# Two linear-attention branches with a gate: the first loads put in one queue, and two input tiles turned before the first product

## The chip, the cores and the metric

The kernel runs on one core of one Trainium2 chip. A core has five engines with a program of their own each: PE (TensorE, matmuls and transposes), DVE (VectorE), ACT (ScalarE), POOL (GpSimd) and SP (SyncE, which here does nothing but issue transfers). Loads and stores are issued from an engine's instruction stream into that engine's own queue; SP's queue is q1 in the profile and ACT's is q10. The packets of both are moved by the same 16 DMA engines. The metric is the device time of one execution in microseconds, as the median of several runs.

## The reference

Two branches A and B have weights of their own and share the input x (2048 rows of 640). Each is a linear attention with 32 heads of 20 columns; a gate mixes the two results.

```
qkv = x @ wqkv                       # 640 -> 3*640, for each branch
pq, pk = phi(q), phi(k)              # phi(t) = (t + 1 if t > 0 else exp(t)) + 1e-6
kv  = sum over s of pk[s] x v[s]     # per head, 20 x 20
z   = sum over s of pk[s]
o   = (pq . kv) / (pq . z + 1e-6)
branch = o @ wo
out = sigmoid((x * gate_w).sum(-1)) * A + (1 - sigmoid(...)) * B
```

## The kernel before

The 2048 rows of x are 16 row tiles of 128, and the 640 columns are 5 column blocks of 128. `XN` holds x as it lies in memory, `XT` holds it transposed (columns on the partitions), and `WK` holds the K part of `wqkv`. K of a row tile is the sum over the five column blocks c of `XT[c, tile]` times `WK[c]`: ten matmuls, a wide one of 512 columns and a narrow one of 128 for each block.

Every piece of work is entered once into a list by helper functions (`dma`, `mms`, `act`, `dve`, `pool`), and each engine then runs its own entries in the order of the list. What an entry reads and writes is declared, and the waits between engines are worked out from that. So the order in the source is the order of every engine and of every DMA queue, and an instruction that waits holds back all that stands behind it on its engine.

The part that the change touches is the start.

- **The loads, L380 to L408.** For the row tiles t = 0 to 3, `load_xn` puts 128 rows of x (160 KB) into SP's queue and `load_wk` puts block t of A's K weights (160 KB) into ACT's queue. Behind them SP's queue gets block 4 of A's K weights, all of B's K weights (800 KB), one column of gate weights, and then fifteen transposing transfers: five column blocks for each of the row groups 4 to 7, 8 to 11 and 12 to 15, which write `XT` directly. The weights of Q and V and the rest of `XN` follow. All transfers are issued at L293.
- **The transposes of the first four tiles.** They are not made by a transfer but on PE: `turn(t, b0)` (L426) waits for `XN` of tile t, makes five PE transposes (L436) into the PSUM banks b0 and b0 + 1, and lets DVE copy column blocks 0 to 2 (L450) and ACT blocks 3 and 4 (L448) into `XT`.
- **The first products.** `ks((t, c), ...)` (L840) adds column block c to K of row tile t through `k_part`: two matmuls a unit, at L304 like all products. Tile t collects in the PSUM pair t, that is in banks 2t and 2t + 1. `fill(bk, n, w)` (L418) makes n matmuls of w columns on constants, whose results nobody reads.
- **The order at the start, L844 to L863.** Twelve fill matmuls, `turn(0)`, one more fill, then products and turns of the tiles 1 to 3 in turn, the remaining products tile by tile, and then `k_tile` for each of the four tiles, which evicts K: ACT takes the exponential (L489) and DVE finishes phi (L500, L505). After that come B's K for the tiles 0 to 3, A's for 4 to 7, B's for 4 to 7 and so on, the Q products, the sums over rows, and the output products with the stores.

The first of A's products for tile 4 needs all five transposing transfers of the row group 4 to 7.

Of the kernel before, what the change touches and what calls it, by code (L numbers as in the profile page):

```python
# [8 lines left out]
ACT = mybir.ActivationFunctionType  # L9
# [197 lines left out]
def bass_gated_mix__linear_attn_block__linear_attn_block__prompt_kernel(  # L207
# [18 lines left out]
    with ExitStack() as es:  # L226
# [45 lines left out]
        def bank(i, lo, hi, p0=0, p1=128):  # L272
            o = 512 * (i % 2)
            return PP[i // 2][p0:p1, o + lo : o + hi]
# [10 lines left out]
        def dma(eng, name, o_ap, i_ap, reads=(), writes=(), transpose=False, noncontig=None):  # L285
            sem = new_sem(name)

            def fn(engobj):
                if noncontig is not None:
                    with nc.allow_non_contiguous_dma(reason=noncontig):  # L290
                        ins = engobj.dma_start(o_ap, i_ap, transpose=transpose)
                else:
                    ins = engobj.dma_start(o_ap, i_ap, transpose=transpose)  # L293
                return ins.then_inc(sem, 16)

            return sch.op(eng, fn, reads=reads, writes=writes, name=name, sem=sem, total=16)

        def mms(steps, reads=(), writes=(), name=""):


            def fn(pe):
                ins = None
                for o, l, r, st, sp, tp in steps:
                    ins = pe.matmul(o, l, r, start=st, stop=sp, tile_position=tp)  # L304
                return ins

            return sch.op("PE", fn, reads=reads, writes=writes, name=name)
# [5 lines left out]
        def act(fn, reads=(), writes=(), name=""):  # L313
            return sch.op("ACT", fn, reads=reads, writes=writes, name=name)

        def dve(fn, reads=(), writes=(), name=""):
            return sch.op("DVE", fn, reads=reads, writes=writes, name=name)
# [7 lines left out]
        def load_xn(eng, t0, t1):  # L325
            dma(
                eng,
                "xn%d" % t0,
                XN[:, t0:t1, :],
                xin[128 * t0 : 128 * t1, :].rearrange("(t p) f -> p t f", p=128),  # L330
                writes=[("XN", t) for t in range(t0, t1)],
            )
# [18 lines left out]
        def load_wk(eng, X, c0, c1):  # L351
            dma(
                eng,
                "wk%s%d" % (X, c0),
                WK[X][:, c0:c1, 0:D],
                wqkv[X][128 * c0 : 128 * c1, D : 2 * D].rearrange("(c p) f -> p c f", p=128),
                writes=[("WK", X, c) for c in range(c0, c1)],
            )
# [10 lines left out]
                fill=0.0,  # L369
# [7 lines left out]
            lambda e: e.activation(SG[:, 2, 0:1], nc.const_aps.tensor(1.0, (128, 1), dt.float32), ACT.Exp),  # L377
            writes=[("SGE", 0)],
        )
        for t in range(4):  # L380
            load_xn("SP", t, t + 1)
            load_wk("ACT", "A", t, t + 1)
        load_wk("SP", "A", 4, NC)
        load_wk("SP", "B", 0, NC)
        dma(
# [35 lines left out]
        def fill(bk, n, w=512):  # L421
            mms(
                [(bank(bk, 0, w), C1[:, 0:128], C1[:, 0:w], True, True, None)] * n,
                writes=[("PS", bk)],
                name="fill",
            )  # L426

        def turn(t, b0):
            for cs, bk in (((0, 1, 2), b0), ((3, 4), b0 + 1)):
                n = len(cs)  # L430
                dst = bank(bk, 0, 64 * n).bitcast(dt.bfloat16)

                def tr(pe, dst=dst, cs=cs):
                    ins = None
                    for i, c in enumerate(cs):
                        ins = pe.transpose(  # L436
                            dst[:, 128 * i : 128 * i + 128],
                            XN[:, t, 128 * c : 128 * c + 128],
                            IDN[:, :],
                        )  # L440
                    return ins

                sch.op("PE", tr, reads=[("XN", t), ("IDN",)], writes=[("PS", bk)], name="tr%d" % t)
                o = XT[:, cs[0] : cs[0] + n, 128 * t : 128 * t + 128]
                i = dst.rearrange("p (c s) -> p c s", c=n)
                ks = [("XT", t, c) for c in cs]
                if n == 2:
                    act(lambda e, o=o, i=i: e.activation(o, i, ACT.Copy), reads=[("PS", bk)], writes=ks)  # L448
                else:
                    dve(lambda e, o=o, i=i: e.tensor_copy(o, i), reads=[("PS", bk)], writes=ks)  # L450
# [4 lines left out]
        def k_part(X, t, pp, cs, first, last):  # L455
            P = PP[pp]
            xs = slice(128 * t, 128 * t + 128)
            bks = [("PS", 2 * pp), ("PS", 2 * pp + 1)]
            for c in cs:
                l = XT[:, c, xs]  # L460
                st, sp = first and c == cs[0], last and c == cs[-1]
                mms(
                    [
                        (P[:, 0:512], l, WK[X][:, c, 0:512], st, sp, None),
                        (P[:, 512:D], l, WK[X][:, c, 512:D], st, sp, None),
                    ],
                    reads=[("XT", t, c), ("WK", X, c)],
                    writes=bks,
                    name="k%s%d" % (X, t),
                )  # L470
# [369 lines left out]
        def ks(*units):  # L840
            for t, c in units:
                k_part("A", t, t, (c,), c == 0, c == NC - 1)

        fill(4, 12, 256)  # L844
        turn(0, 6)
        fill(4, 1)
        ks((0, 0))
        turn(1, 6)
        ks((0, 1), (1, 0), (1, 1))
        turn(2, 6)  # L850
        ks((0, 2), (1, 2), (2, 0), (2, 1), (2, 2))
        turn(3, 6)
        ks((0, 3), (0, 4))
        ks((1, 3), (1, 4), (2, 3), (2, 4))
        ks(*[(3, c) for c in range(NC)])
        for t in range(4):
            k_tile("A", t, True)
# [120 lines left out]
```

## Time and profile before

| what | us |
|---|---|
| median of three runs | 193.09 (192.46 to 193.37) |
| the profiled execution | 192.72 |
| its span, first to last instruction of the program | 191.0 |
| PE busy | 185.7 (97% of the span) |
| DVE busy | 124.5 (65%) |
| ACT busy | 75.5 (40%) |
| POOL busy | 44.6 (23%) |
| moved by DMA | 19.07 MB, 100 GB/s on average |
| granted TensorE clock | 1.00 throughout |

All times in the text are microseconds from the start of the span of this profiled execution. A transfer has an issue (the time at which SP or ACT hands it to its queue) and a landing (the time at which the last of the 16 DMA engines has reported its share). A row of the timeline gives the start, the duration, the engine, the line, the operation, the tile written and the tiles read, the number of instructions that it stands for, and in square brackets how long the engine had been idle before it and what ended that. A row for a stretch of time gives the busy time of engines in it, the granted clock, the share of time that the DMA engines were busy, and the GB/s that they moved.

### The profile page before, as it was taken

The numbers are of one execution on the slowest core, as the hardware profiler recorded it, in microseconds if no ns is written. First come the engines' busy times: TensorE is split into PE (matmuls) and PEld (weight loads), VectorE is DVE, ScalarE is ACT, GpSimd is POOL, SyncE is SP. The second block draws the span as 40 slices with busy tenths as digits, with TensorE's granted clock in tenths as the row PEclk, the third lists the DMA queues.
The fourth block names the chain that finished last, engine by engine and source line by source line (L and its number), as shares of the span: only waits on it lengthen the run. The fifth ranks groups of instructions, "written<-read, shape, count | busy, mean of one in ns | idle before, by whom it ended". The sixth has DMA issues, their size and how long they took to land.

```text
span 191.0 us, 3548 instructions
## 1 busy us (share of the span) xinstructions
PE 185.7 (97%) x1402; PEld 102.7 (54%) x1428; DVE 124.5 (65%) x211; ACT 75.5 (40%) x131; POOL 44.6 (23%) x38
## 2 busy tenths in 40 slices
PE   7999999999999999999999999999999999999994
PEld 4555555555545454545454457555557555555553
DVE  0299899998997674857767663891332856582663
ACT  3366464656633533533444422212114533223302
POOL 1000223244224746556637430000000000000000
PEclk9999999999999999999999999999999999999999
DMA  6994549996310000011000004029694011111113
GB/s 185 303 130 85 98 99 316 367 363 205 85 27 0 0 3 0 10 55 43 3 0 2 0 3 107 3 48 219 181 298 195 3 69 69 37 69 69 72 69 103
DMA packets 22785, 19.07 MB, mean 100 GB/s; under 512 B 10288, under 2 KB 22000, under 8 KB 22768
## 3 DMA queue, kind: packets, MB, share of 16 engines
q1 hardware_dynamic: 21904, 18.08, 33.5%
q10 hardware_dynamic: 864, 0.76, 1.2%
q8 instruction: 11, 0.18, 0.4%
q14 instruction: 6, 0.05, 0.1%
HBM read 12.94 MB, written 3.93 MB: 88 GB/s over the span
## 4 chain that ended last, share of the span: by engine, by line
PE 90%; DVE 3%; DMA 2%; issue 1%; ACT 1%; SPq 0%; DVEq 0%
PE ps L304 90%; DMA XN<-in_A_x_dram 2%; DVE PKA L505 2%; DVE EK L500 1%; ACT WPB L752 1%; DVE OSTG L810 0%; SPq L293 0%; PE ps L436 0%; DVE PKB L505 0%; ACT EK L489 0%; DVEq L948 0%; DVEq L159 0%
## 5 line engine op out<-in xcount | busy, mean ns | idle before, releaser
L530 ACT ACTIVATE EQ<-ps 128x512 bf16<-128x512 f32 x40 | 23.9, 597 | 34.1 <-PE ps L304 34.0
L489 ACT ACTIVATE EK<-ps 128x640 bf16<-128x640 f32 x32 | 22.3, 703 | 16.2 <-PE ps L304 15.3
L535 DVE TENSOR_SCALAR EQ<-EQ 128x512 bf16<-128x512 bf16 x40 | 15.3, 383 | 17.8 <-ACT EQ L530 17.1
L582 POOL TENSOR_TENSOR ZS<-ZS,PKA 128x640 f32<-128x640 f32 x13 | 18.7, 1439 | 27.3 <-DVE PKB L505 12.1
L810 DVE SCALAR_TENSOR_TENSOR OSTG<-ps,SG,PKB 128x640 bf16<-128x640 f32 (+3 forms) x18 | 14.5, 810 | 15.9 <-PE ps L304 15.9
L304 PE MATMUL ps<-PKA,XN 128*128 128x128 bf16 (+1 forms) x156 | 24.5, 297 | 0.2
L789 ACT ACTIVATE PKB<-ps,SG 128x640 f32<-128x640 f32 (+2 forms) x17 | 13.0, 764 | 28.7 <-PE ps L304 28.7
L304 PE MATMUL ps<-WPA,PQA 128*128 128x128 bf16 (+1 forms) x155 | 23.3, 297 | 0.4 <-ACT WPB L752 0.2
L304 PE MATMUL ps<-WPB,PQB 128*128 128x128 bf16 (+4 forms) x162 | 23.4, 294 | 0.2
L304 PE MATMUL ps<-XT,WQB 128*128 128x512 bf16 x99 | 23.2, 379 | 0.1
L304 PE MATMUL ps<-WKA,XT 128*128 128x128 bf16 (+1 forms) x157 | 22.7, 298 | 0.4
L304 PE MATMUL ps<-XT,WQA 128*128 128x512 bf16 x97 | 22.6, 379 | 0.2
L304 PE MATMUL ps<-WKB,XT 128*128 128x512 bf16 (+1 forms) x157 | 22.1, 298 | 0.2
L582 POOL TENSOR_TENSOR ZS<-ZS,PKB 128x640 f32<-128x640 f32 x13 | 19.1, 1469 | 13.5 <-DVE PQB L540 11.0
L304 PE MATMUL ps<-PKB,XN 128*128 128x512 bf16 (+1 forms) x156 | 21.7, 297 | 0.3 <-issue 0.2
L304 PEld LDWEIGHTS ps<-PKA,XN 128*128 128x128 bf16 x160 | 13.1, 98 | 11.7
L304 PEld LDWEIGHTS ps<-WPB,PQB 128*128 128x128 bf16 x165 | 13.4, 98 | 8.9
L304 PEld LDWEIGHTS ps<-WPA,PQA 128*128 128x128 bf16 x160 | 12.9, 98 | 9.7
L304 PEld LDWEIGHTS ps<-WKB,XT 128*128 128x128 bf16 x160 | 12.4, 97 | 9.6
L304 PEld LDWEIGHTS ps<-WKA,XT 128*128 128x128 bf16 x160 | 12.3, 98 | 9.7 <-DVE XT L450 0.9
L304 PEld LDWEIGHTS ps<-PKB,XN 128*128 128x128 bf16 x160 | 12.2, 98 | 9.5 <-issue 0.3
L500 DVE TENSOR_SCALAR EK<-EK 128x640 bf16<-128x640 bf16 x32 | 14.6, 457 | 2.6 <-ACT EK L489 2.4
(63 smaller groups left out, 153.3 us busy)
## 6 DMA issues: line engine op xcount, KB each, us to landing
out_dram<-OSTG SPq DMA_DIRECT2D x15, 160.0 KB, 1.8
XN<-in_A_x_dram SPq DMA_DIRECT2D x3, 640.0 KB, 8.8
PKA<-rsA SPq DMA_DIRECT2D x3, 384.0 KB, 4.0
XT<-rsB SPq DMA_DIRECT2D x3, 384.0 KB, 5.8
WKB<-in_B_wqkv_dram SPq DMA_DIRECT2D x1, 800.0 KB, 7.4
WQA<-in_A_wqkv_dram SPq DMA_DIRECT2D x1, 800.0 KB, 6.3
WVA<-in_A_wqkv_dram SPq DMA_DIRECT2D x1, 800.0 KB, 10.5
WQB<-in_B_wqkv_dram SPq DMA_DIRECT2D x1, 800.0 KB, 11.3
```

The lines of the kernel that those rows point to most:

```text
L304: ins = pe.matmul(o, l, r, start=st, stop=sp, tile_position=tp)
L489: lambda e: e.activation(EK[:, slot, :], P[:, 0:D], ACT.Exp),
L500: lambda e: e.tensor_scalar(EK[:, slot, :], EK[:, slot, :], 1.0, EPS, op0=ALU.min, op1=ALU.add),
L505: lambda e: e.scalar_tensor_tensor(out=PK[X][:, t, :], in0=P[:, 0:D], scalar=0.0, in1=EK[:, slot, :], op0=ALU.max, op1=ALU.add),
L530: lambda e: e.activation(EQ[:, slot, :], bank(bk, 0, 512), ACT.Exp),
L535: lambda e: e.tensor_scalar(EQ[:, slot, :], EQ[:, slot, :], 1.0, EPS, op0=ALU.min, op1=ALU.add),
L582: lambda e: e.tensor_tensor(out=o, in0=a, in1=PK[X][:, t, :], op=ALU.add),
L752: lambda e, o=o, p=p, j=j: e.tensor_copy(o, p) if j else e.activation(o, p, ACT.Copy),
L789: lambda e, lo=lo, hi=hi: e.activation(TA[:, t % 5, lo:hi], PP[pp][:, lo:hi], ACT.Copy, scale=SG[:, 0, t : t + 1]),
L810: lambda e, lo=lo, hi=hi, p=p: e.scalar_tensor_tensor(out=OSTG[:, slot, lo:hi], in0=p, scalar=SG[:, 1, t : t + 1], in1=TA[:, t % 5, lo:hi] ...
```

## The change

The transfers of the first tiles, which were issued pairwise by SP and ACT, are now all issued by SP, in the order x0, x1, K-weight block 0, block 1, x2, block 2, x3, block 3, and then block 4 as before. On PE, `turn(1)` moves ahead of the first product, with its transposes in the banks 4 and 5 in place of 6 and 7; the fills go to bank 0 in place of bank 4, eleven of 256 columns in place of twelve before `turn(0)`, and one of 256 columns behind `turn(1)`. The first four units of products come in another order. From `turn(2)` on, the sequence of PE is the same as before, unit by unit: the two `ks` lines at its end are written as one, and give the same order.

```diff
-        for t in range(4):
-            load_xn("SP", t, t + 1)
-            load_wk("ACT", "A", t, t + 1)
+
+        load_xn("SP", 0, 1)
+        load_xn("SP", 1, 2)
+        load_wk("SP", "A", 0, 1)
+        load_wk("SP", "A", 1, 2)
+        load_xn("SP", 2, 3)
+        load_wk("SP", "A", 2, 3)
+        load_xn("SP", 3, 4)
+        load_wk("SP", "A", 3, 4)
         load_wk("SP", "A", 4, NC)
         load_wk("SP", "B", 0, NC)
...
-        fill(4, 12, 256)
+        fill(0, 11, 256)
         turn(0, 6)
-        fill(4, 1)
-        ks((0, 0))
-        turn(1, 6)
-        ks((0, 1), (1, 0), (1, 1))
+        fill(0, 1)
+        turn(1, 4)
+        fill(0, 1, 256)
+        ks((0, 0), (1, 0), (0, 1), (1, 1))
         turn(2, 6)
         ks((0, 2), (1, 2), (2, 0), (2, 1), (2, 2))
         turn(3, 6)
-        ks((0, 3), (0, 4))
-        ks((1, 3), (1, 4), (2, 3), (2, 4))
+        ks(*[(t, c) for t in range(3) for c in (3, 4)])
         ks(*[(3, c) for c in range(NC)])
```

## The prediction, made before the change was run

> **What bounds the kernel now.** I read the page first, for the engine that sets the end.
>
> ```profile
> span 191.0 us, 3548 instructions
> PE 185.7 (97%) x1402; PEld 102.7 (54%) x1428; DVE 124.5 (65%) x211; ACT 75.5 (40%) x131; POOL 44.6 (23%) x38
> PE 90%; DVE 3%; DMA 2%; issue 1%; ACT 1%; SPq 0%; DVEq 0%
> ```
>
> PE is busy for 97% and makes 90% of the chain that ended last, so a change at the start is worth what it moves in PE's first unbroken stretch. Where that begins is read from PE's weight loads (PEld), one row of which stands ahead of each group of matmuls.
>
> ```profile
> 3.55 0.31 PEld L436 LDWEIGHTS ps<-IDN,XN 128*128 128x128 bf16 x5 [0.48 <-DMA XN<-in_A_x_dram]
> 4.38 0.11 PEld L304 LDWEIGHTS ps<-WKA,XT 128*128 128x128 bf16 x2 [0.46 <-DVE XT L450]
> 4.71 0.28 PEld L436 LDWEIGHTS ps<-IDN,XN 128*128 128x128 bf16 x5 [0.22 <-DMA XN<-in_A_x_dram]
> 5.50 0.39 PEld L304 LDWEIGHTS ps<-WKA,XT 128*128 128x128 bf16 x4 [0.40 <-DVE XT L450]
> 6.41 0.28 PEld L436 LDWEIGHTS ps<-IDN,XN 128*128 128x128 bf16 x5 [0.52 <-DMA XN<-in_A_x_dram]
> ```
>
> PE waits five times: for x0, the copy of `XT` 0, x1, the copy of `XT` 1, and x2. Behind 6.41 it starts a matmul at every slot: the four units before ended at 6.06, `turn(2)` starts at 6.41, unit (0,2) at 6.70, `turn(3)` at 8.06, the first product with B's weights (B0) at 11.27, and A's tile 4 (A4) at 16.78. As the order from `turn(2)` on is unchanged, **the gain is how much earlier PE gets to unit (0,2) than 6.70, less any wait that appears at B0 or A4**. Nothing later is near: the Q weights land at 33.58 for a first use at 49.4.
>
> What feeds it is the transfers. Their rows by stretch (the last number is GB/s):
>
> ```profile
> 2.00:3.00 1.00, 1.00 (x7) 1.00 0.89 216
> 3.00:4.00 1.00, 1.00 (x9) 1.00 1.08 376
> 4.00:5.00 1.00, 0.87 (x9) 1.00 1.04 332
> 5.00:6.00 1.00, 0.93 (x8) 1.00 0.86 170
> 6.00:7.00 1.00, 0.81 (x10) 1.00 0.99 339
> ```
>
> With 20 KB moved before 2.0, the sums are 236 KB at 3.0, 612 at 4.0, 944 at 5.0, 1114 at 6.0 and 1453 at 7.0. The engines are full, except from 5 to 6, where packets of q1 took up to 1007 ns for a usual 55: a slow stretch of about 4.75 to 6.1.
>
> Three landings matter later; the last number is us from issue to landing, for x2 (issued 1.71), B's K weights (3.14) and the fifth transposing transfer (11.97).
>
> ```profile
> XN<-in_A_x_dram SPq DMA_DIRECT2D x1, 160.0 KB, 4.7
> WKB<-in_B_wqkv_dram SPq DMA_DIRECT2D x1, 800.0 KB, 7.4
> XT<-in_A_x_dram SPq DMA_TRANSPOSE x1, 4.6
> ```
>
> To the hundredth they land at 6.37, 10.50 and 16.57: PE's spare time is 0.77 at B0 and **only 0.21 at A4**.
>
> **The fills and PE's own work.** Eleven plus one of 256 columns and one of 512 are the same number as before; a fill of 256 takes a slot of 0.213 (starts 1.220, 1.433, 1.647), and the slots lie in waits. Bank 0 in place of 4 and banks 4 and 5 for `turn(1)` add no wait: tile 2's products, the next users of banks 4 and 5, come after the copies of tile 1 by over 0.5. `turn(1)` no longer stands behind unit (0,0). Cost 0; if the cover of the wait were gone, 0.1 for the fill behind `turn(1)`.
>
> **When the tiles land in one queue.** A tile is 164 KB. In order of landing now: x0 first at 3.51, when 428 KB were moved, 2.6 tiles; block 0 second at 3.91, 578 KB, 3.5 tiles; block 1 fourth at 4.86, 897 KB, 5.5 tiles. So a tile lands when about 1.5 more than its own place are moved (the DMA engines run unevenly). For x2 and block 2 (6.37 and 6.59, places 5 and 6) it is 2.5 and 2.0, as tiles of places 7 and 8 were moved beside them in the other queue. In one queue nothing behind them goes ahead on the same engine; I take 1.5, bounds 1.0 and 2.0. On the sums above this gives x1 (place 2, 3.5 tiles, 573 KB) 3.90 in place of 4.67, block 0 4.38, block 1 4.87, x2 (1065 KB) 5.71, block 2 (1229 KB) 6.34, x3 6.82, block 3 7.27, block 4 7.69.
>
> PE then: a wait ends 0.04 behind a landing (6.37 to 6.41) and `XT` is there 0.79 behind the start of a turn (4.71 to 5.50). `turn(1)` 3.94, unit (0,0) 4.42 when block 0 is in, (1,0) 4.73, then 0.27 for each of four units to 5.54; `turn(2)` 5.75; (0,2) waits for block 2 until 6.38. **Gain 0.32.** x3 and blocks 3 and 4 have 0.6 to 0.7 to spare now and land earlier.
>
> This holds if the slow stretch stays at its time. No row tells its cause. If it is tied to SP's next issues (the gate column at 3.61 and the first transposing transfer at 4.18), these move 1.8 later, and so does it, behind block 2. With 332 GB/s kept from 4 on, x2 lands at 5.36, block 2 at 5.86, and (0,2) starts at 5.90: gain 0.80. B0 would come at 11.27 - 0.80 = 10.47 and find B's weights at 10.50 plus 0.04 (the same bytes stand ahead of them): 0.73.
>
> **The four issues moved to SP.** SP issues one every 0.46 to 0.47 (1.26, 1.71, 2.19, 2.66), so the K weights of B, the gate column and the fifteen transposing transfers are issued 4 times that later: 1.85 in all, or 1.77 by the four durations of about 0.44. ACT loses its four issues beside the table load, and has nothing to do until 4.08: no gain. What the shift costs is read from SP's own rows.
>
> ```profile
> 3.14 0.43 SPq L293 DMA_DIRECT2D WKB<-in_B_wqkv_dram  x1
> 4.18 2.89 SPq L293 DMA_TRANSPOSE XT<-in_A_x_dram  x1
> 9.36 1.26 SPq L293 DMA_TRANSPOSE XT<-in_A_x_dram  x1
> 11.97 1.26 SPq L293 DMA_TRANSPOSE XT<-in_A_x_dram  x1
> 32.71 2.16 SPq L293 DMA_DIRECT2D WQB<-in_B_wqkv_dram  x1
> ```
>
> An issue of one shape takes 0.43 with little queued and 2.16 with three loads ahead: SP is held while the queue is deep. The first transposing issue takes 2.89, the second 2.20 (7.12 to 9.32) and those behind 1.26. So 1.63 and 0.94, together 2.57, are waiting for the queue to drain, which depends on bytes moved and not on when SP asks. Starting at 6.0, the first still ends at 6.0 + 1.26 = 7.26 for now 7.07, the second at 9.32 again; the third to fifth are unmoved. I take 0 to 0.2 for the delay; the other bound is the full 1.8. At A4 the landing of the fifth is late by itself: it takes 4.6 from its issue where the seventh (15.51) takes 3.5, since from 14 to 15 the queue moves 28 GB/s, beside and behind a 16 KB instruction packet from 13.12 to 14.42. Eleven such packets for PE's some 2,830 instructions look like PE's own fetch; then it comes earlier as PE does, and A4's spare time is kept. If it stays at its time, A4 waits until 16.61 and the whole gain is 0.17.
>
> **Sum.** 0.32 or 0.73 by the place of the slow stretch, cut to 0.17 if the fifth transfer stays: I take the middle, 0.45. The span goes from 191.0 to 190.55 and its execution from 192.72 to 192.27; the median stands 0.37 above that execution, so it goes from 193.09 to **192.64**. A difference under 0.5%, 0.97 us, is about what a measurement of this kernel cannot tell from no change.
>
> **Rivals.**
> *The transposing transfers slip (slower).* If the 2.89 and 2.20 are the price of these two issues themselves and not waiting, SP's whole 1.77 comes through: the fifth lands at 18.34, A4 starts at 18.38 for 16.78, and nothing gained before it counts: 1.60 lost, 194.7. It decides from a slip of 0.21 plus whatever was gained; a half slip costs 0.7. For it: the second issue is long although the queue behind it was then mostly one load. Against it: the same operation takes 1.26 twelve times, and its only other long one (2.20 at 13.27) spans the stretch of 28 GB/s.
> *The start gets rid of the slow stretch and of the unevenness.* With 1.0 tile in place of 1.5 and 332 GB/s throughout, x1 lands at about 3.46, block 2 at 5.37, (0,2) starts at 5.44: gain 1.26. The 162 KB not lost (332 less 170) bring B's weights to about 10.0, just in time for B0 at 10.01. 191.8. For it: q10's packets were almost all at 55 ns, so one queue alone may not stall as two do; from 7 to 8 q1, by then all but alone, moved 387 GB/s. Against it: q1 had packets of 450 to 624 ns before q10 moved any (2.0 to 2.3).
> *Nothing.* With 2.0 tiles behind its place block 2 lands at 6.0 + (1311 - 1114)/339 = 6.58, as now: 193.1.
>
> [...]
>
> **How the numbers follow.** The forecast has 0.37, nothing 0.19, the slip 0.21, the clean start 0.23. Same takes the forecast, nothing, and a small part of both others: 0.53. Faster has 0.26 and slower 0.21. The likeliest case's own range is 192.3 to 193.0; with the others it is 191.8 (the clean start) to 194.5 (the slip, nearly whole).
>
> **What would show it.** Right: x1 lands by 4.1, `turn(2)` starts by 5.9 and (0,2) by 6.4, the first transposing issue starts near 6.0 and ends near 7.3, and the third starts within 0.3 of 9.36. Wrong: a weight load of A4 that waits for a DMA of `XT` (the slip), (0,2) at 6.6 or later (nothing), or no stretch under 250 GB/s before 8 (the clean start).

## The result, and the profile after

The changed kernel is slower. Its median is 194.06 us (193.71 to 194.63, six runs) where the kernel before took 192.93 (192.31 to 193.37, six runs): a ratio of 1.0065 with an interval of 1.005 to 1.008, or 1.13 us. The forecast was 192.64. The profiled execution of the changed kernel took 194.63, the longest of its six, and that of the kernel before, 192.72, lay below its median, so the two traces stand 1.91 apart where the medians stand 1.13 apart. The place of the loss can be read from them, its usual size only from the medians.

Three lines of the page after, against those shown of before:

```profile
span 192.9 us, 3575 instructions
PE 188.1 (98%) x1428; PEld 103.6 (54%) x1428; DVE 124.4 (65%) x211; ACT 75.6 (39%) x131; POOL 44.6 (23%) x38
PE 89%; SPq 7%; DMA 2%; issue 1%; DVE 0%; DVEq 0%
```

The third line is the change in one number: SP's issues (SPq) now make 7% of the chain that ended last, where they made 0%. Before, the chain left the transfers at 6.41 and ran along PE, with a stretch of evictions on ACT and DVE from 9.08 to 15.63. Now it follows SP much further, in order of time (start, duration, what):

```profile
6.09 1.87 SPq L293
...
8.01 3.39 SPq L293
...
11.44 1.26 SPq L293
...
12.74 1.26 SPq L293
...
14.05 4.39 DMA XT<-in_A_x_dram
18.44 0.33 issue
18.77 170.84 PE ps L304 x1304
```

Five transposing issues, of which the second took 3.39 us where a free one takes 1.26, then the fifth transfer, which lands at 18.44, and behind it PE without a break. On PE's side (weight loads; lines behind the loads have moved by six, so that `turn` is at L442):

```profile
3.09 0.52 PEld L442 LDWEIGHTS ps<-IDN,XN 128*128 128x128 bf16 x5 [0.23 <-DMA XN<-in_A_x_dram]
5.31 0.14 PEld L304 LDWEIGHTS ps<-WKA,XT 128*128 128x128 bf16 x2 [0.64 <-DVE XT L456]
6.88 0.32 PEld L442 LDWEIGHTS ps<-IDN,XN 128*128 128x128 bf16 x5
7.16 1.24 PEld L304 LDWEIGHTS ps<-WKA,XT 128*128 128x128 bf16 x10
12.68 5.46 PEld L304 LDWEIGHTS ps<-WKB,XT 128*128 128x128 bf16 x40 [1.01 <-DVE PKA L511]
18.74 0.78 PEld L304 LDWEIGHTS ps<-WKA,XT 128*128 128x128 bf16 x5 [0.59 <-issue]
```

`turn(0)` starts 0.46 earlier than before (3.55), but (0,2) starts 0.51 later: its weight load at 7.16 for 6.65, and its first matmul, the 6.70 of the prediction, 0.05 behind that in both. Two waits are new: 1.01 ahead of B0 and 0.59 ahead of A4. The first is put down to DVE, but the eviction that B0 needs there had ended at 11.51 (in the kernel before, B0 started before the next one ended); B's K weights landed at 12.57. The second is the fifth transposing transfer.

From A4 to the end every kernel of this study takes 174.16 to 174.22 us, whatever happened before. **So all differences lie ahead of A4.** And where no transfer is late, A4 stands 10.08 behind (0,2), which is PE's own work between them (10.07 to 10.08 in six of the kernels below). That splits the loss of this execution: 0.51 is there at (0,2), and 18.74 - 7.16 - 10.08 = 1.50 us more are waits for transfers. I call the second part the late share. B0 stands 4.62 to 4.63 behind (0,2) where nothing is late and here 5.52, so 0.90 of the late share is the wait for B's K weights and 0.60 the one for the fifth transposing transfer.

SP handed the weights over at 5.04 in place of 3.14, and began with the transposing transfers at 6.09 in place of 4.18:

```profile
5.04 0.43 SPq L293 DMA_DIRECT2D WKB<-in_B_wqkv_dram  x1
6.09 11.26 SPq L293 DMA_TRANSPOSE XT<-in_A_x_dram  x6
```

And the DMA engines moved less, in rows of one microsecond (the last number is GB/s):

```profile
3.00:4.00 1.00, 1.00 (x8) 1.00 0.88 246
4.00:5.00 1.00, 1.00 (x7) 1.00 0.75 242
5.00:6.00 1.00, 0.71 (x4) 1.00 0.95 305
6.00:7.00 1.00, 1.00 (x9) 1.00 0.80 248
7.00:8.00 1.00, 1.00 (x13) 1.00 0.94 294
8.00:9.00 1.00, 1.00 (x12) 1.00 0.95 306
```

With 309 KB at 3.0 the sums are 555 at 4.0, 797 at 5.0, 1102 at 6.0 and 1350 at 7.0, where the kernel before had 612, 944, 1114 and 1453. Its one slow row (170) has become six rows of 242 to 306. In the packets this is seen one by one. A packet of 1280 bytes usually takes 52 to 55 ns; in both kernels single ones took several hundred to over a thousand (up to 1007 ns before, 1082 after), and I say of these that they hung. Three packets of the changed kernel (start, duration, end, bytes):

```
 8.341  1082 ns   9.423   1280
 9.521   368 ns   9.889   1280
10.120  2391 ns  12.511    256
```

B's K weights are 640 packets of 1280 bytes, or 40 for each of 16 engines if they are shared evenly. The rows don't number the engines, so what follows is an estimate: 40 packets at 52 ns behind 9.889 end at 11.97, and the last four packets of the weights end 52 ns apart, the last at 12.02. Meanwhile packets of the first transposing transfer are moved (256 bytes, usually 18 ns, and the 4-byte reports ahead of them), and the 25 of these that were held, begun between 10.1 and 11.7, end together at 12.49 to 12.53. The weights' landing comes with them (16 reports from 9.51 to 12.57, before 10.25 to 10.50), and SP's second issue ends at 11.40 in place of 9.32. My reading is that an engine late with its share held all of this back; no row shows it.

### The profile page after: what moved, and what is told of

Read it like the earlier page. It is cut to its first block, busy times and chain, and to the rows that moved or that the text cites. A ratio compares the mean times of both kernels' runs of the same rounds, so it can differ in the third digit from the quotient of the medians.

```text
span 192.9 us, 3575 instructions
## 1 busy us (share of the span) xinstructions
PE 188.1 (98%) x1428; PEld 103.6 (54%) x1428; DVE 124.4 (65%) x211; ACT 75.6 (39%) x131; POOL 44.6 (23%) x38
## 4 chain that ended last, share of the span: by engine, by line
PE 89%; SPq 7%; DMA 2%; issue 1%; DVE 0%; DVEq 0%
PE ps L304 89%; SPq L293 6%; DMA XT<-in_A_x_dram 2%; DVE OSTG L816 0%; SPq L291 0%; DVEq L953 0%; DVEq L159 0%
## 5 line engine op out<-in xcount | busy, mean ns | idle before, releaser
L304 PE MATMUL ps<-PKA,XN 128*128 128x512 bf16 (+1 forms) x160 | 24.8, 299 | 0.0
L304 PE MATMUL ps<-WPA,PQA 128*128 128x512 bf16 (+1 forms) x160 | 24.2, 299 | 0.0
L304 PE MATMUL ps<-WKA,XT 128*128 128x512 bf16 (+1 forms) x160 | 23.2, 303 | 0.7 <-DMA XT<-in_A_x_dram 0.4
L304 PE MATMUL ps<-WPB,PQB 128*128 128x512 bf16 (+4 forms) x165 | 23.9, 295 | 0.0
L304 PE MATMUL ps<-XT,WQA 128*128 128x512 bf16 x100 | 23.1, 379 | 0.0
L304 PE MATMUL ps<-PKB,XN 128*128 128x512 bf16 (+1 forms) x160 | 22.2, 299 | 0.0
L304 PEld LDWEIGHTS ps<-PKA,XN 128*128 128x128 bf16 x160 | 13.1, 98 | 11.7
L304 PEld LDWEIGHTS ps<-WKA,XT 128*128 128x128 bf16 x160 | 12.5, 99 | 10.6 <-issue 1.1
```

## The experiments

Six theories are named by letters in the expectations. **D**: one queue drains more slowly, its packets hang and its engines become uneven (in E1 and E5 because it is one queue, whatever its lead; from E9 on because it is fed only just ahead). **S**: SP hands over B's K weights and the transposing transfers too late. **P**: PE's new order costs the time. Later also **L** (the weights need a lead of some microseconds), **W** (the transposing transfers alone are late) and **G** (handing over the gate column and the transposing transfers is what makes packets hang).

Medians are in us, ratios are against the kernel before on the same chip, with 95% intervals. Where a number of a profile stands beside a median, it belongs to one execution.

### The two halves of the change

**E1**, the loads of after with PE's order of before:

```diff
-        for t in range(4):
-            load_xn("SP", t, t + 1)
-            load_wk("ACT", "A", t, t + 1)
+        load_xn("SP", 0, 1)
+        load_xn("SP", 1, 2)
+        load_wk("SP", "A", 0, 1)
...
+        load_wk("SP", "A", 3, 4)
```

> The loads of after (one queue), the order of PE of before. Theory D (one queue drains more slowly: when a packet of it hangs on a DMA engine, that engine has no other queue to go on with): the loss of after, 0.8 to 1.4 us, with B's K weights landing after 11.5. Theory S (draining is the same, but SP hands over B's K weights and the transposing transfers 1.9 us later): the same 0.8 to 1.4. Theory P (the order of PE does it): within 0.3 us of before.

**E2**, the loads of before with PE's order of after:

```diff
-        fill(4, 12, 256)
+        fill(0, 11, 256)
         turn(0, 6)
-        fill(4, 1)
-        ks((0, 0))
-        turn(1, 6)
-        ks((0, 1), (1, 0), (1, 1))
+        fill(0, 1)
+        turn(1, 4)
+        fill(0, 1, 256)
+        ks((0, 0), (1, 0), (0, 1), (1, 1))
...
```

> The loads of before (two queues), the order of PE of after. Theories D and S: within 0.4 us of before, as the start on PE is bound by the same landings; theory P: 0.8 to 1.4 us slower.

E1 took 194.01 (1.0063, interval 1.004 to 1.0085), the whole loss. E2 took 192.89 (1.0006, 0.9994 to 1.0018). P falls: PE's order costs nothing and brings nothing, with the loads of before (E2 against before) and with those of after (after, 194.06, against E1), and the loads alone cost it all.

### One queue or two, and the hand-over

**E3**, after with the same loads in the same order, issued by SP and ACT in turn:

```diff
-        load_xn("SP", 0, 1)
-        load_xn("SP", 1, 2)
-        load_wk("SP", "A", 0, 1)
...
+        for i, (load, t) in enumerate(
+            [(load_xn, 0), (load_xn, 1), (load_wk, 0), (load_wk, 1), (load_xn, 2), (load_wk, 2), (load_xn, 3), (load_wk, 3)]
+        ):
+            eng = ("SP", "ACT")[i % 2]
...
```

> The loads of after in the same order, but issued by SP and ACT in turn, so in two queues with four issues each, and the order of PE of after. Theories D and S: the loss goes, within 0.4 us of before; B's K weights land before 10.9. If the order of need as such is what costs, it stays 0.8 to 1.4 us slower.

**E4**, the kernel before with four loads of 4 KB on SP ahead of B's K weights, which shift SP's later issues as the change does. They fill a tile that nothing reads:

```diff
         load_wk("SP", "A", 4, NC)
+        for i in range(4):
+            dma("SP", "late%d" % i, LATE[:, 16 * i : 16 * i + 16], A_wo[0:128, 16 * i : 16 * i + 16], writes=[("LATE", i)])
         load_wk("SP", "B", 0, NC)
```

> Before, with four tiny loads (4 KB each, into a tile that nobody reads) issued by SP between block 4 and B's K weights, so that SP hands over everything behind them some 1.9 us later, while the two queues for the first tiles stay. Theory S: the loss of after, 0.8 to 1.4 us. Theory D: within 0.4 us of before, B's K weights landing before 10.9.

E3 took 193.05 (1.0004, 0.9994 to 1.0015): with two issuers the order of after costs nothing. Its rows by stretch, to be put beside those of after:

```profile
3.00:4.00 1.00, 0.89 (x8) 1.00 1.03 360
4.00:5.00 1.00, 1.00 (x10) 1.00 1.02 342
5.00:6.00 1.00, 1.00 (x8) 1.00 0.98 306
6.00:7.00 1.00, 1.00 (x13) 1.00 1.04 353
```

B's K weights, handed over at 3.15, land at 10.29. E4 took 194.20 (1.0063, 1.004 to 1.0086), as much as after, with the tiles of before in two queues. Its rows stay at 311 GB/s or more until 6.0, and fall only then, when the last tiles are all that is left:

```profile
5.00:6.00 1.00, 0.93 (x10) 1.00 0.92 311
6.00:7.00 1.00, 0.93 (x10) 1.00 1.07 233
7.00:8.00 1.00, 1.00 (x9) 1.00 0.98 114
8.00:9.00 1.00, 1.00 (x13) 1.00 0.61 214
```

A packet of E4 hung for 1841 ns. The weights, handed over at 5.03, land at 12.08. As far as this S holds, and D's limits for this run (within 0.4 us, landing before 10.9) are missed: shifting SP's later issues reproduces the loss without the one queue. But the slow rows are also those in which the four added loads are moved (512 packets of 32 bytes, from 6.10 to 7.48), so E4 can't tell the two apart. E6 below adds no load.

### Is it lateness as such?

**E6** and **E7**, the kernel before with B's K weights and all behind them held until ACT has copied tile 0, or tile 1 (the declared read makes SP wait; the loads behind move with it). The diff is E6's; in E7 the read is ("XT", 1, 3), and `rest()` stands behind `turn(1, 6)`:

```diff
-        load_wk("SP", "B", 0, NC)
...
+        def rest():
+            load_wk("SP", "B", 0, NC, [("XT", 0, 3)])
...
         turn(0, 6)
+        rest()
```

> Before, with two queues, where SP waits for ACT's copy of tile 0 before it issues B's K weights and all that is behind them: handed over at about 4.5 us for now 3.1, with no transfer added. Theory L: 0.3 to 1.0 us slower, B's K weights land between 11 and 12. Theory D: within 0.3 us of before, as the queues come to these weights only at 6.5 to 7.

> The same with the wait for ACT's copy of tile 1, so that SP hands over B's K weights at about 5.6 us (5.0 in after). Theory L: 1.2 to 2.5 us slower, more than with the wait for tile 0. Theory D: within 0.4 us of before.

**E8**, the kernel before with only the transposing transfers (and what is behind them) held until tile 1 is copied:

```diff
+                        reads=[("XT", 1, 3)],
                         writes=[("XT", t, c) for t in range(4 * b, 4 * b + 4)],
                         transpose=True,
```

> Before, where only the transposing transfers wait for ACT's copy of tile 1 (first issue at about 5.6 us for now 4.2); B's K weights and the gate column are issued as before. Theory L: within 0.3 us of before, since the first two issues were held by the full queue for 2.6 us in any case. If it is the late hand-over of the transposing transfers that costs in after: 0.8 to 1.4 us slower.

E6 hands the weights over at 4.70 and took 193.40 (1.0046, 1.0025 to 1.0067): with two queues and nothing added, the late hand-over makes the kernel slower. L had this time right, and D not. E7 hands them over at 6.21, later than the changed kernel does, and took 192.82 (1.0000, 0.9986 to 1.0014). So lateness alone doesn't explain the loss, and L falls with it: later was better. Their rows, E6's first:

```profile
12.59 5.46 PEld L304 LDWEIGHTS ps<-WKB,XT 128*128 128x128 bf16 x40 [1.32 <-DVE EK L474]
19.47 2.62 PEld L304 LDWEIGHTS ps<-WKA,XT 128*128 128x128 bf16 x18 [1.42 <-issue]
```

```profile
6.21 0.39 SPq L293 DMA_DIRECT2D WKB<-in_B_wqkv_dram  x1
11.41 5.49 PEld L304 LDWEIGHTS ps<-WKB,XT 128*128 128x128 bf16 x40
16.86 5.09 PEld L304 LDWEIGHTS ps<-WKA,XT 128*128 128x128 bf16 x36
```

In E7 the tiles were still moving at the hand-over, but their last packet ended at 6.71 and the first of the weights began at 7.27, so that the engines came to the weights from an empty queue; they began them together and reported them from 10.46 to 11.07. In E6's profile (195.42, the longest of its twelve) there is no such gap, a packet hung for 1560 ns and the weights landed at 12.49.

E8 took 192.88 (0.9998, 0.9984 to 1.0011). SP's row and PE's:

```profile
5.68 7.08 SPq L293 DMA_TRANSPOSE XT<-in_A_x_dram  x5
```

```profile
10.98 5.49 PEld L304 LDWEIGHTS ps<-WKB,XT 128*128 128x128 bf16 x40
16.43 5.48 PEld L304 LDWEIGHTS ps<-WKA,XT 128*128 128x128 bf16 x40
```

The first transposing issue starts 1.50 later than before (5.68 for 4.18) and yet neither B0 nor A4 waits at all. W falls.

### What makes the packets hang

**E9**, the changed kernel with the gate column and the transposing transfers held until tile 3 is copied, and **E10**, the same with B's K weights held too. In both `rest()` issues all that is held; it begins with these lines in E10, and in E9 with the gate column, which there has the read:

```diff
+        def rest():
+            load_wk("SP", "B", 0, NC, [("XT", 3, 3)])
+            dma(
+                "SP",
+                "gw",
...
         turn(3, 6)
+        rest()
```

> After, where SP waits for ACT's copy of tile 3 (about 9.4 us) before it issues the gate column and the transposing transfers; the nine first transfers and B's K weights are issued as in after. Read from the trace: when B's K weights land. Theory G (packets hang because SP is handing over the gate column and the transposing transfers, with many small pieces each, while the DMA engines work on the same queue): before 11.0, no packet of these weights over 0.6 us. Theory D (one queue that is fed only just ahead of the DMA engines): 12.0 or later as in after, with packets over 1 us. The whole time is longer in both, by 1 to 3 us, since the transposing transfers are issued 3 us later.

> After, where SP waits for ACT's copy of tile 3 before it issues B's K weights and all that is behind them: the nine first transfers are alone. Read from the trace: when x2, block 2 and block 4 land (6.20, 6.60 and 8.96 in after; 6.37, 6.59 and 7.98 in before). Theory D: as in after, block 4 at 8.5 or later. Theory G, and any in which the later issues are at fault: x2 by 5.6, block 4 by 7.6. The whole time is 3 to 5 us longer, as B's weights come late.

**E11**, the kernel before with the weights behind the copy of tile 0, as E6, and the gate column with what follows behind the copy of tile 2 (the reads are ("XT", 0, 3) and ("XT", 2, 3)):

```diff
         turn(0, 6)
+        load_wkb()
...
         turn(2, 6)
+        rest()
```

> Before, with two queues, where SP waits for ACT's copy of tile 0 before it issues B's K weights (4.7 us) and for that of tile 2 (about 7) before the gate column and the transposing transfers. Theory G: B's K weights land by 10.6, where 12.5 was seen with the transposing transfers right behind them, and the time is that of before, or up to 0.5 us less. Theory D or one in which the lead of these weights counts: they land after 11.5, 0.3 to 1 us slower.

E9 took 194.74 in its one execution. SP's rows show that nothing was handed over behind the weights until 9.01:

```profile
5.04 0.43 SPq L293 DMA_DIRECT2D WKB<-in_B_wqkv_dram  x1
9.01 0.37 SPq L291 DMA_DIRECT2D WKB<-in_gate_w_dram  x1
```

Still a packet hung for 1640 ns, from 8.20 to 9.84, and the weights landed at 12.53. By this one execution G falls. E10 has nothing but the nine tiles in its one queue:

```profile
3.00:4.00 1.00, 1.00 (x9) 1.00 0.86 237
4.00:5.00 1.00, 0.60 (x8) 1.00 0.97 301
5.00:6.00 1.00, 1.00 (x8) 1.00 0.88 246
6.00:7.00 1.00, 0.65 (x8) 1.00 0.82 264
...
12.00:13.00 1.00, 0.00 (x0) 1.00 1.06 394
```

The nine tiles by themselves move at 237 to 301 GB/s, much as in the changed kernel, and the weights, begun at an empty queue, reach 394. So the slow rows need nothing behind the tiles. But x2 landed at 5.95 and block 4 at 8.09, between the limits of both theories (D: block 4 at 8.5 or later; G: x2 by 5.6, block 4 by 7.6), so the landings don't settle it, and block 4 came only 0.11 later than before. E10 took 197.12, as its weights land only at 14.01 and PE then runs at half pace (a granted clock of 0.50 from 15.0 to 17.0, last section).

E11 took 193.37 (1.0031, 1.0017 to 1.0045): the weights, handed over at 4.83, land at 11.22, again between the limits (10.6 and 11.5). B0 doesn't wait for them (11.52, which is (0,2) + 4.62); its loss is a wait at A4 for the fifth transposing transfer, which it hands over later by its own hold and which lands at 17.63. That the weights land earlier here than in E6 rests on one profile of each, and the medians of both are level.

### One queue, fed well ahead

**E5** and once more as **E12**, the changed kernel with its nine tiles in five transfers, all on SP:

```diff
...
+        load_xn("SP", 0, 2)
+        load_wk("SP", "A", 0, 2)
+        load_xn("SP", 2, 4)
         load_wk("SP", "A", 2, 3)
-        load_xn("SP", 3, 4)
-        load_wk("SP", "A", 3, 4)
-        load_wk("SP", "A", 4, NC)
+        load_wk("SP", "A", 3, NC)
```

> After, still one queue and the order of need, but in five transfers in place of nine (x0 with x1, blocks 0 and 1, x2 with x3, block 2, blocks 3 and 4), so that SP hands over B's K weights at 3.1 us as before and not at 5.0. Theory L (a transfer moves fast only if it was handed over some 3 us before the DMA engines come to it; handed over later, its packets hang): the loss goes, from 0.6 us faster to 0.3 slower than before, B's K weights land before 10.8. Theory D (one queue drains more slowly whatever its lead): 0.8 to 1.4 us slower, as after.

> The kernel of E5 once more, for a second profiled execution, since E5's was the fastest of its twelve (192.83) and so does not show what its median (193.40) pays for. If a queue handed work well ahead is safe (lead of 4 tiles or more at 3 to 5 us), B's K weights land by 10.6 again, A4 starts by 17.0 and the execution takes at most 193.1; the remaining 0.38% of E5 would then lie outside the start. If one queue is uneven by itself, whatever its lead, the weights land after 11.0 with 20 or more packets over 300 ns, A4 starts as much later as the execution is over 192.83, and the time is 193.3 to 194.

E5 took 193.40 (1.0038, 1.0018 to 1.0057): of the 0.65% of after, it keeps 0.38%. That is 0.57 us and lies between the ranges of L (at most 0.3 slower) and D (0.8 to 1.4). Its profiled execution was the fastest of its twelve (192.83), and E12 took 193.19 in its one, so E12's limits of 193.1 and 17.0 were missed by a little (A4 at 17.26), and the other theory's landing after 11.0 by more: the weights landed at 10.48, and from 3 to 10 us 13 packets of tiles and weights took over 300 ns, none over 724. PE's rows of E12:

```profile
3.98 0.45 PEld L438 LDWEIGHTS ps<-IDN,XN 128*128 128x128 bf16 x5 [1.13 <-DMA XN<-in_A_x_dram]
7.18 1.24 PEld L304 LDWEIGHTS ps<-WKA,XT 128*128 128x128 bf16 x10
11.81 5.49 PEld L304 LDWEIGHTS ps<-WKB,XT 128*128 128x128 bf16 x40
17.26 1.73 PEld L304 LDWEIGHTS ps<-WKA,XT 128*128 128x128 bf16 x13
```

There is no wait ahead of B0 or A4: 17.26 - 7.18 = 10.08. What E12 loses is lost before (0,2): `turn(0)` starts at 3.98 where the kernel before has 3.55, as tiles 0 and 1 land together (3.94), and PE came to full pace only at 6.09 (see the last section). One queue with its work handed over early doesn't make the weights late in these two executions; its larger first transfer makes the start late. This speaks against D in its first form, one queue whatever its lead.

### The runs side by side

From each profile: the lead, which is the tiles of 164 KB that were handed over at least 1 us ago less the tiles moved, at 3, 4, 5 and 6 us; when B's K weights were handed over and when they landed; the start of (0,2) and of A4; and the late share, A4 - (0,2) - 10.08.

| kernel | lead at 3, 4, 5, 6 | weights | (0,2) | A4 | late share | ratio |
|---|---|---|---|---|---|---|
| before | 4.7, 5.4, 8.3, 7.3 | 3.14 to 10.50 | 6.65 | 16.78 | 0.05 | |
| E2 | 4.8, 5.5, 8.3, 5.9 | 3.15 to 9.98 | 7.09 | 17.17 | 0.00 | 1.0006 |
| E3 | 4.3, 5.1, 8.0, 6.2 | 3.15 to 10.29 | 6.37 | 16.44 | -0.01 | 1.0004 |
| E8 | 4.6, 5.3, 8.1, 6.7 | 3.14 to 9.95 | 6.35 | 16.43 | 0.00 | 0.9998 |
| E5 | 4.7, 5.4, 8.7, 6.7 | 3.32 to 10.36 | 6.82 | 16.90 | 0.00 | 1.0038 |
| E12 | 4.7, 5.5, 8.9, 7.0 | 3.32 to 10.48 | 7.18 | 17.26 | 0.00 | (same kernel) |
| after | 1.2, 1.7, 2.2, 2.4 | 5.04 to 12.57 | 7.16 | 18.74 | 1.50 | 1.0065 |
| E1 | 1.3, 2.1, 2.6, 2.5 | 5.05 to 12.20 | 8.53 | 18.94 | 0.33 | 1.0063 |
| E9 | 1.2, 2.0, 2.3, 2.5 | 5.04 to 12.53 | 6.71 | 18.83 | 2.04 | one run |
| E4 | 4.6, 5.3, 3.3, 1.5 | 5.03 to 12.08 | 6.74 | 18.33 | 1.51 | 1.0063 |
| E6 | 4.5, 5.2, 3.1, 6.0 | 4.70 to 12.49 | 6.77 | 19.47 | 2.62 | 1.0046 |
| E11 | 4.9, 5.5, 3.3, 6.1 | 4.83 to 11.22 | 6.90 | 17.94 | 0.96 | 1.0031 |
| E7 | 4.6, 5.2, 3.0, 1.0 | 6.21 to 11.07 | 6.79 | 16.86 | -0.01 | 1.0000 |
| E10 | 1.3, 1.9, 2.1, 2.5 | 9.07 to 14.01 | 6.81 | 21.18 | 4.29 | one run |

Weights handed over by 3.32 land by 10.50 and nothing is late. Handed over between 4.70 and 5.05, they land at 11.22 to 12.57, in one queue or two, and the late share is 0.33 to 2.62 (in E9 and E11 a part of it is the transposing transfers, which these runs hold back). Handed over at 6.21, with the tiles gone before their first packet, they land at 11.07, just in time. The rows are single executions: those of E3, E5 and E8 are the fastest of their twelve, and those of after, E1 and E6 the longest of theirs, which makes the contrast larger than it usually is. The profiles of E2, E4 and E7 lie within 0.3 us of their medians and show the same two groups; the usual size is the ratio. E1 shows the other way of paying: there `turn(1)` stands behind unit (0,0), whose block 0 landed at 5.34, PE stood idle from 4.52 to 5.48 and then ran at half pace until 9.17 (units 0.52 to 0.54 apart, for 0.27), and most of its loss is already in (0,2).

No version is faster than the kernel before: E2, E3, E7 and E8 are level with it.

## Why the prediction was wrong

**PE sets the end from (0,2) on, and only B0 and A4 can add a wait.** Right as a frame: the time from A4 on is constant, and A4 is (0,2) + 10.08 or what a transfer makes of it. The forecast came out on the wrong side because both terms were wrong.

**The failed step: "the same bytes stand ahead of them".** The prediction put B's K weights at 10.50 again, although SP was to hand them over four issues later: it took their landing to follow from the bytes ahead of them, and gave the time of the hand-over no cost. They landed at 12.57, 2.07 later; B0 waited 0.90, and through SP's second transposing issue, of 3.39, A4 waited 0.60 more. The runs show that the hand-over counts by itself. In E6, with two queues and nothing added, the same bytes stand ahead as well; handed over at 4.70, the weights land at 12.49 and the kernel is 0.46% slower. In E5 and E12, with one queue but an early hand-over (3.32), they land by 10.48. E7 shows that it isn't a matter of lateness as such: handed over at 6.21, with the last packet of the tiles ended at 6.71 and the first of the weights begun at 7.27, they land at 11.07 and nothing is late.

The pace was not the same either. SP hands over 164 KB every 0.47 us, 349 GB/s, where the full rows of before moved 332 to 387. With one issuer the queue is never more than 2.4 tiles ahead up to 6 us, and it moved 242 to 306 GB/s; with two issuers it was 4.7 to 8.3 ahead. The prediction had SP's interval of 0.46 to 0.47 in its hands and used it to say when the issues end, but did not set 164 KB per interval against what the engines move. How much this adds to the late hand-over is not separated: after loses 0.65%, E6 0.46% and E4, with its added loads, 0.63%. For the same loads in the same order, one issuer gave a ratio of 1.0065 (after) and two gave 1.0004 (E3).

**The landing rule of 1.5 tiles.** It was applied to before's curve, and failed with it, except at the front: x1 landed at 3.54 (forecast 3.90), but block 0 at 5.21 (4.38), block 1 at 5.67 (4.87), x2 at 6.20 (5.71) and block 4 at 8.96 (7.69). That in one queue nothing behind a tile goes ahead of it, as it assumed, fits the landings: in after the nine come in the order of their issue (3.05, 3.54, 5.21, 5.67, 6.20, 6.60, 7.02, 7.77, 8.96). On the curve of after the rule fails too: x1, block 0, block 1, x2 and block 4 landed 0.7, 2.2, 2.1, 2.0 and 2.8 tiles behind their own places. The promise that `turn(2)` starts by 5.9 and (0,2) by 6.4 was missed: 6.88 and 7.21.

**A unit takes 0.27.** This was read from the profile of before, where PE ran at full pace from 3.55 on. In the profile of after, units started up to 0.53 apart until 6.4; see the last section. It is most of the 0.51 at (0,2): E9, with the loads and the order of after up to there and block 0 at 5.25, was at full pace from 5.28 and had (0,2) at 6.71, 0.06 later than before. E2, with the loads of before, had it at 7.09. So this part varies from one execution to the next, and the loads alone explain little of it.

**The four issues moved to SP.** The absorption was right as a mechanism: E8 shows 1.50 of lateness swallowed whole. In after the first transposing issue started at 6.09, as forecast (6.0), but ended at 7.96 (7.26): the absorption had the proviso that the queue drains as before. It did not, and so the second issue was held for 3.39 until 11.40, and the third started at 11.44, not at 9.36.

**PE's order and the fills cost 0.** Right (E2).

**The rivals.** The sign promised for the slip, a weight load of A4 that waits for a transfer of `XT`, came true, and its loss of 1.60 (194.7) is of the order of the 1.13 between the medians. Its reason did not come true: it made the long issues a price of the issues themselves, and E8 moves them without any loss. So that it named the right direction is luck. The sign of "nothing", (0,2) at 6.6 or later, came true as well, without its time. The clean start asked whether one queue runs more evenly than two, and in after it did not: from 3 to 10 us 17 packets of tiles and weights took over 300 ns, as many as before, but spread over the whole stretch instead of lying mostly between 4.7 and 6.1. Its sum also took half a tile where its text says one; with one, by its own figures, block 2 would land at 5.61 and the gain would be about 1.05, not 1.26.

**What stays open.** What a hung packet waits for: no row names it. Nor why packets hang at just such a time; the lead goes with the loss in most of these profiles, but before's own packets hung (up to 1007 ns) with a lead of 5 to 8 tiles, and E7's (up to 895 ns) and E10's (up to 1055 ns) at the start of the weights behind an empty queue, and before and E7 lost nothing by it. Nor is it shown how the loss of after divides between the late hand-over and the short queue. That E5 loses its 0.38% by its larger first transfers is read from two profiles, both faster than its median, and was not tried by itself.

## What to carry to other kernels

Before several issuers of loads are merged into one, work out when the one issuer will hand over the first large transfer behind the small ones, and give that time a cost of its own: in E6 the weights landed at 12.49 and before at 10.50, with the same bytes ahead of them. Look at what holds its issuer, too: here the second transposing issue took 3.39 where a free one takes 1.26. It also helps to divide the bytes of a transfer by the issuer's interval and compare that with what the DMA engines move in the profile: here the quotient (349 GB/s) was not clearly larger than what the full rows moved (332 to 387), and the queue was never more than 2.4 tiles ahead up to 6 us; what that costs without a late hand-over behind it, no run shows. And ask of every duration taken for PE's first microseconds whether PE was already at full pace in that execution.

## What the hardware showed beyond this

**PE came to full pace at times from 3.55 to 9.17.** In after, weight loads of one shape take 147 to 152 ns at first and then mostly 98, and transposes start 107 ns apart and then 56. The step came at 3.55 in the profile of before, at 6.6 in after, and between 3.87 and 9.17 in the others; in E5 and E12, the same kernel, at 5.16 and 6.09, which goes with most of the 0.36 between their (0,2). The latest, 9.17, is E1's, where PE had stood idle from 4.52 to 5.48. The granted clock reads 1.00 there all the same, but in E10, where PE stood idle for 2.54 us ahead of B0 (11.61 to 14.15), it does show it (start and end, sum, PE busy, clock, DMA share, GB/s):

```profile
14.00:15.00 1.00, 0.85 (x3) 0.55 1.36 202
15.00:16.00 1.00, 1.00 (x4) 0.50 0.70 148
16.00:17.00 1.00, 1.00 (x8) 0.50 2.35 42
17.00:18.00 1.00, 1.00 (x4) 0.74 0.28 28
18.00:19.00 1.00, 1.00 (x10) 1.00 0.54 108
```

From B0 to A4 it took 7.06 in place of the 5.45 of E8 and E12, so 1.6 of E10's late share is PE at half pace and not the transfer. The trace's records of E10's clock change at 3.87 (to 1.00), 14.11 (to 0.50) and 17.52 (to 1.00); at 14.11 PE had been idle for 2.50 us. In before the first record, to 1.00, is at 3.66 and in after at 6.41, next to the steps in pace. What sets these times, no run shows.

**The first transposing transfer was held until behind B's K weights.** Its held packets end together, about half a microsecond behind the last packet of those weights: at 12.49 to 12.53 behind 12.02 in after, at 10.24 to 10.27 behind 9.71 in before, at 12.00 to 12.04 behind 11.58 in E4 and at 12.36 to 12.40 behind 11.90 in E6. The longest took 2391, 984, 1979 and 2658 ns, where a free packet of 256 bytes takes 18. That one late engine stopped the others is an inference: no row numbers the engines.
